# A decode kernel's output row moved from four spread partitions to eight neighbouring ones

## The chip, the cores and the metric

The kernel runs on one core of one Trainium2 chip. Times are device microseconds (us) of one execution. Ratios are the mean time of one kernel's fast runs over the mean of the other's fast runs of the same rounds, so they are not quite the ratio of the medians quoted beside them. A span in a profile runs from the first to the last instruction and is about 1.3 us shorter than the device time of the same run. Single executions of one kernel differ by about 0.3 us. So each claim rests on two things: the medians of repeated runs, and the last few microseconds of the trace, where single durations repeat to about 0.02 us.

## The reference

One token of attention with 32 query heads over a cache of 65,536 positions, a small gated MLP, and a gate that mixes the two. What matters here is the last line: two products that end in the same 1024 outputs.

```python
def reference(A_x, A_k_cache, A_v_cache, A_wq, A_wo, B_x, B_w_in, B_w_sp, B_b_sp, B_w_out, gate_w):
    ...                                   # q = x @ wq, softmax(q k / sqrt(128)) v per head
    a = o.reshape(1, 1, 4096) @ A_wo      # A_wo is 4096 x 1024, 8 MB
    b = (z1 * g_b) @ B_w_out              # the MLP, 1792 x 1024
    return g * a + (1 - g) * b            # 1024 numbers in bf16
```

## The kernel before

All inputs are loaded once, in one stream of large loads on the SP queue: keys, values, and at the very end `A_wo` in pieces. The last three pieces hold five, two and one of eight rows of weights per partition. The engines are written for the raw language, with semaphores planned by a small recorder.

The output `o @ A_wo` is one row, so a matmul uses one column of weights (`ovec`, one value per partition) and streams the rows of `A_wo` past it. The code places the matmuls in four groups of 32 columns (`tile_position`), and the groups run side by side: in the trace the four matmuls of a row of weights start within 0.02 us of each other, and the next row follows after 0.11 us at full clock, 0.21 at half. Each group writes to its own 32 partitions of PSUM (`fb[32*q:32*q+1]`). The kernel gives each group a quarter of the 1024 outputs, so the sums end on partitions 0, 32, 64 and 96, with 256 columns each:

```python
for c in range(c0, c1):                       # rows of weights per partition
    for q in range(4):                        # four column groups
        o = DO * (c - c0) + QW * q            # QW = 256
        e.matmul(fb[32*q:32*q+1, 0:QW], ovec[:, 8*i+c:8*i+c+1], sl[:, o:o+QW], start=False, ...,
                 tile_position=(0, 32*q))
...
P("DVE", lambda e: e.tensor_copy(orow[0:97, :], fb[0:97, 0:QW]), w=["orow", "fb"])   # PSUM -> SBUF
store()
# the store's source: four partitions, every 32nd
osrc = bass.AP(tensor=arena, offset=OFF["OROW"], ap=[[32 * NA, 4], [1, QW]])
```

The same store is also issued once early, of zeros, just before the last load. The MLP's product is summed in rows of 512 into `ob`, and four small fp32 matmuls with the vector `e4` spread it into the four rows of `fb`.

## Time and profile before

| | before |
|---|---|
| median of the runs | 382.32 us (382.23 to 382.40, six runs) |
| bytes read | 162 MB, 426 GB/s over the span |
| busy: DMA, PE, DVE | over 90% in 39 of 40 slices, 60%, 54% |
| last landing of weights to end of span | 2.60 us |

The page of the profile, its header and the rows of 40 equal slices. A digit is the busy share of a slice in tenths:

```profile
span 381.1 us, 2468 instructions
...
PE 229.2 (60%) x1383; PEld 55.5 (15%) x793; DVE 204.5 (54%) x162; ACT 22.2 (6%) x23; POOL 7.5 (2%) x35
...
DMA  9999999999999999999999999999999999999995
...
q8 instruction: 8, 0.13, 0.1%
```

DMA is full from the first slice to the last but one. No compute engine is near that. So the load stream sets the time, and a change after it can only win in what follows the last landing. The last line is the queue that the page calls "instruction" (packets, MB, share of the span of all 16 engines): eight packets.

The chain of work that ended last, for the last 15 us (start us, length us, what):

```profile
345.52 31.08 DMA arena<-in_A_wo_dram
...
376.74 1.73 PE fbt L718 x28
378.47 0.03 issue
378.50 0.41 PE fbt L718 x4
...
379.00 0.42 DVE arena L724
```

The timeline of the same stretch (start us, length us, engine, line, operation, operands, count, and in brackets the idle time before it and what ended it), with the early store of zeros first:

```profile
346.47 0.63 SPq L354 DMA_DIRECT2D out_dram<-arena  x1
...
378.50 0.09 PEld L718 LDWEIGHTS fbt<-arena 128*1 128x1 bf16 x4 [0.52 <-DMA arena<-in_A_wo_dram]
379.00 0.42 DVE L724 CAST arena<-fbt 97x256 bf16<-97x256 f32 x1 [9.98 <-PE fbt L718]
379.45 0.54 SPq L354 DMA_DIRECT2D out_dram<-arena  x1
```

So the tail reads like this. The last row of weights lands at 378.45 (from the record of landings). PE starts at 378.50 and releases DVE, which copies from 379.00 for 0.42 us. SP issues the store at 379.45 for 0.54 us. The store lands at 381.05. That last stretch is SP's final wait (waited for, us in total, times, longest):

```profile
SPq L121 <- DMA out_dram<-arena: 1.1, 1, 1.1
```

PE's clock in the last two 3.4 us windows was half speed (columns: busy time and count of PE, weight loads, DVE, ACT, POOL; PEclk; DMA share; GB/s):

```profile
374.10:377.60 3.50, 1.67 (x40) 0.78 (x28) 0.00 (x0) 0.00 (x0) 0.00 (x0) 0.51 0.78 315
377.60:381.00 3.40, 1.25 (x20) 0.19 (x12) 0.42 (x1) 0.00 (x0) 0.00 (x0) 0.50 0.02 6
```

### The profile page before, as it was taken

Reading aid. Unit: us, or ns where it says so; the run is one execution under the profiler, and the core shown is the slowest. Engines: PE = TensorE matmul, PEld = TensorE weight load, DVE = VectorE, ACT = ScalarE, POOL = GpSimd, SP = SyncE. Lnnn points to the kernel's source line nnn. Section 1 sums busy time; section 2 is a strip of 40 time slices with the busy share of each in tenths; the row PEclk is TensorE's granted clock in tenths of the full one; section 3 lists DMA queues with packets and bytes.
Section 4 is the critical chain, followed back from the end, with each engine's and each line's share of the span. In section 5 each row is a group of like instructions: output and inputs, shape, how many; then the busy total and the mean of one; then the engine's idle time right before and its main releaser. Section 6 shows DMA issues by size and latency. Waiting matters only on the chain.

```text
span 381.1 us, 2468 instructions
## 1 busy us (share of the span) xinstructions
PE 229.2 (60%) x1383; PEld 55.5 (15%) x793; DVE 204.5 (54%) x162; ACT 22.2 (6%) x23; POOL 7.5 (2%) x35
## 2 busy tenths in 40 slices
PE   0050487566558924893887238952995984549373
PEld 0010011111111200121111001220121111212031
DVE  3111596778489525956882249745875871402020
ACT  1000000010420000002000000022000000220000
POOL 4000000000000000000000000000000000000000
PEclk9997599698959975999798858985998896959776
DMA  9999999999999999999999999999999999999995
GB/s 440 434 433 413 426 387 437 440 492 420 428 433 392 426 442 440 433 420 433 454 428 440 440 440 440 421 433 440 392 420 439 457 433 426 426 408 433 423 430 223
DMA packets 4237, 162.15 MB, mean 426 GB/s; under 512 B 508, under 2 KB 516, under 8 KB 772
## 3 DMA queue, kind: packets, MB, share of 16 engines
q1 hardware_dynamic: 4192, 162.01, 98.7%
q8 instruction: 8, 0.13, 0.1%
q10 hardware_dynamic: 36, 0.00, 0.0%
q14 instruction: 1, 0.01, 0.0%
HBM read 162.01 MB, written 0.00 MB: 425 GB/s over the span
## 4 chain that ended last, share of the span: by engine, by line
DMA 63%; DVE 18%; PE 17%; issue 1%; ACTq 0%; SPq 0%; DVEq 0%
DMA arena<-in_A_k_cache_dram 41%; DVE arena L490 15%; DMA arena<-in_A_v_cache_dram 10%; DMA arena<-in_A_wo_dram 8%; PE scp L250 5%; DMA arena<-in_B_b_sp_dram 5%; PE scp L252 5%; PE obt L250 3%; PE obt L252 3%; DVE arena L527 1%; PE fbt L718 1%; ACTq L276 0%; DVE arena L563 0%; DVE arena L561 0%; SPq L377 0%
## 5 line engine op out<-in xcount | busy, mean ns | idle before, releaser
L490 DVE STREAM_TRANSPOSE arena<-arena 128x2048 f32<-128x2048 f32 x64 | 142.8, 2283 | 45.9 <-DMA arena<-in_A_k_cache_dram 31.3
L250 PE MATMUL scp<-arena 128*128 128x512 bf16 x256 | 108.9, 425 | 84.9 <-DVE arena L490 84.9
L252 PE MATMUL scp<-arena 128*128 128x512 bf16 x256 | 107.7, 421 | 0.0
L250 PE MATMUL obt<-arena 128*64 128x512 bf16 (+2 forms) x334 | 62.8, 416 | 21.3 <-DMA arena<-in_A_v_cache_dram 21.3
L252 PE MATMUL obt<-arena 128*64 128x512 bf16 (+2 forms) x334 | 61.9, 410 | 0.0
L250 PEld LDWEIGHTS scp<-arena 128*128 128x128 bf16 x256 | 26.9, 105 | 194.4 <-issue 99.5
L527 DVE STREAM_TRANSPOSE arena<-arena 128x2048 bf16<-128x2048 bf16 x7 | 16.2, 2311 | 31.3 <-PE obt L252 29.1
L250 PEld LDWEIGHTS obt<-arena 128*64 128x64 bf16 (+1 forms) x334 | 18.3, 113 | 74.5 <-issue 56.9
L522 ACT ACTIVATE arena<-arena 128x2048 bf16<-128x2048 f32 x8 | 16.0, 2003 | 218.1 <-DVE arena L519 195.0
L507 DVE TENSOR_SCALAR_CACHE_REDUCE arena<-scp 128x2048 f32<-128x2048 f32 x8 | 18.3, 2292 | 16.0 <-PE scp L252 16.0
L568 PE MATMUL mbt<-arena 128*128 128x128 bf16 x16 | 2.2, 286 | 13.6 <-DVE arena L563 13.6
L530 DVE STREAM_TRANSPOSE arena<-arena 128x1024 bf16<-128x1024 bf16 x2 | 2.5, 1245 | 12.7 <-PE obt L252 12.7
L718 PE MATMUL fbt<-arena 128*1 128x256 bf16 x128 | 6.6, 370 | 4.1 <-DMA arena<-in_A_wo_dram 4.0
L556 DVE RECIPROCAL arena<-mbt 128x1 f32<-128x1 f32 x4 | 0.6, 140 | 15.7 <-PE mbt L551 15.7
L478 POOL COPY arena<-arena 32x32 bf16<-32x32 bf16 x16 | 3.3, 204 | 236.3 <-PE scp L252 210.9
L519 DVE TENSOR_REDUCE arena<-mbt 128x1 f32<-128x32 f32 x4 | 0.8, 192 | 13.3 <-PE mbt L516 13.3
L420 PE MATMUL scp<-arena 8*128 8x1 bf16 x8 | 0.6, 197 | 10.8 <-DVE arena L415 10.8
L425 PE MATMUL mbt<-arena 1*128 1x2 bf16 x1 | 0.2, 158 | 10.4 <-DMA arena<-in_B_b_sp_dram 10.4
L724 DVE CAST arena<-fbt 97x256 bf16<-97x256 f32 x1 | 0.4, 425 | 10.0 <-PE fbt L718 10.0
L427 DVE COPY arena<-mbt 128x2 f32<-128x2 f32 x1 | 0.2, 159 | 10.4 <-PE mbt L425 10.4
L718 PEld LDWEIGHTS fbt<-arena 128*1 128x1 bf16 x128 | 3.3, 103 | 7.2 <-DMA arena<-in_A_wo_dram 3.4
L415 DVE TENSOR_TENSOR arena<-arena 8x1024 bf16<-8x1024 bf16 x1 | 1.2, 1211 | 4.9 <-DMA arena<-in_A_x_dram 4.9
(88 smaller groups left out, 48.9 us busy)
## 6 DMA issues: line engine op xcount, KB each, us to landing
arena<-in_A_k_cache_dram SPq DMA_DIRECT2D x6, 4096.0 KB, 33.2
arena<-in_A_v_cache_dram SPq DMA_DIRECT2D x2, 4096.0 KB, 26.9
arena<-in_B_w_in_dram SPq DMA_DIRECT2D x1, 7168.0 KB, 31.0
arena<-in_A_wo_dram SPq DMA_DIRECT2D x3, 2048.0 KB, 34.4
arena<-in_B_w_out_dram SPq DMA_DIRECT2D x1, 3584.0 KB, 21.8
arena<-in_A_wo_dram SPq DMA_DIRECT2D x1, 1280.0 KB, 31.1
arena<-in_A_wo_dram SPq DMA_DIRECT2D x1, 512.0 KB, 31.8
arena<-in_A_wo_dram SPq DMA_DIRECT2D x1, 256.0 KB, 31.3
```

Of the source, the lines that this page charges most:

```text
L250: return e.matmul(*a, **kw)
L252: one = e.matmul(*a, **kw).ins
L415: P("DVE", lambda e: e.tensor_tensor(vw(xm, 0, [[128, 8], [1, 128]], 0, 8), vw(xrow, 0, [[0, 8], [1, 128]], 0, 8), vw(idb, 0, [[1, 8], [0, ...
L478: P("POOL", lambda e, pb=pb: e.tensor_copy(vw(qpad, 24 + 32 * pb, [[QP, 4], [1, 8]], 32 * pb, 32), vw(qall, 8 * g, [[32, 4], [1, 8]], 32 * ...
L490: P("DVE", lambda e: e.transpose(ktb(i).bitcast(F32), sl[:, 4096 * p:4096 * (p + 1)].bitcast(F32)), r=keys[4 * p:4 * p + 4], w=[("kt", i % ...
L507: P("DVE", lambda e: e.tensor_scalar(scs(j), scp[:, :], 0.0, None, op0=ALU.add, op1=ALU.max, accum_out=maxc[:, j:j + 1]), w=[("sc", j % 2) ...
L519: P("DVE", lambda e: e.tensor_reduce(gcol(g, K_NB), mb[:, 0:32], AXX, ALU.min), w=[("nb", g), "mb"])
L522: P("ACT", lambda e: e.activation(psb2, scs(j), ACTF.Exp, bias=gcol(j // 2, K_NB), scale=SCALE, accum_out=lp[:, j:j + 1]), r=[("sc", j % 2 ...
L527: P("DVE", lambda e: e.transpose(ptsb2, psb2), r=["psb"], w=[("ptsb", 0), ("ptsb", 1)])
L530: P("DVE", lambda e: e.transpose(ptsb(n), ab("PSB", 1024, 1024 * (n % 2))), r=["psb"], w=[("ptsb", n % 2)])
L568: ins = e.matmul(mb[:, 0:128], sel[:, 128 * c:128 * (c + 1)], osc[:, 128 * c:128 * (c + 1)], start=(c == 0), stop=(c == 3))
L718: ins = e.matmul(fb[32 * q:32 * q + 1, 0:QW], ovec[:, 8 * i + c:8 * i + c + 1], sl[:, o:o + QW], start=False, stop=(i == 3 and c == 7), ti ...
```

## The change

The intent: end with eight rows of 128 columns on eight partitions that follow one another, 28 to 35, so that the copy is short and the store is a block of neighbours. These partitions lie in two column groups, so only two groups of PE work; each matmul takes a weight load of 32 columns. A window into a zero-padded vector (`ovz`) puts the one useful column at the right place. To make up for PE's lost half, the first half of `A_wo` is summed in rows of 512 over four groups and spread into the eight rows later, and ten filler matmuls (`spin`) are meant to keep PE busy so that its clock stays up.

```diff
-    QW = DO // 4
+    NW = 8
+    QW = DO // NW
+    W0 = 32 - NW // 2
...
-    osrc = bass.AP(tensor=arena, offset=OFF["OROW"], ap=[[32 * NA, 4], [1, QW]])
+    osrc = orow[W0:W0 + NW, :]
...
+    SLOTS = []
+    for h in range(NW // 2):
+        SLOTS += [(h, 0, W0 + h), (NW // 2 + h, 1, h)]        # (which 128 outputs, column group, row in it)
+    def wo_rows(i):                     # first half of A_wo: rows of 512, four groups, into scp
...
+    def wo_piece(i, c0=0, c1=8):        # second half: rows of 128 straight into fb
+        ...
+                for s, b, j in SLOTS:
+                    z = 31 + 32 * (8 * i + c) - j
+                    ins = e.matmul(fb[32 * b:32 * (b + 1), 0:QW], ovz[:, z:z + 32], sl[:, o:o + QW], ...,
+                                   tile_position=(0, 32 * b))
...
     out_first(3)
+    wo_rows(0)
     out_rest(3)
+    wo_rows(1)
+    spin(4)
+    spread(scp, [KSC(0)], False)        # ACT copy 97x1024, then eight fp32 matmuls
+    spin(3)
+    wo_piece(2)
+    spin(3)
+    for c0, c1 in WO_CUT:
+        wo_piece(3, c0, c1)
-    P("DVE", lambda e: e.tensor_copy(orow[0:97, :], fb[0:97, 0:QW]), w=["orow", "fb"])
+    P("DVE", lambda e: e.tensor_copy(orow[0:W0 + NW, :], fb[0:W0 + NW, 0:QW]), w=["orow", "fb"])
```

## The prediction

> **What bounds the kernel now.** The page's header and its row of 40 slices: 162 MB at a mean of 426 GB/s, DMA 9 tenths busy in every slice but the last, PE 60%, DVE 54%. The chain of waits over the last 80 us is almost only DMA: value cache until 339.5, output weights until 376.6. So the load queue sets the time, and only what follows the last landing can be saved. Read from the landings and instruction times: the last piece of the output weights (one of eight rows) lands at 378.45 us; its four 128*1 by 256 matmuls start at 378.50 and release DVE at 378.94 (0.41 us, clock at half); the 97x256 copy takes 0.42; the store is issued at 379.45 for 0.54 and lands at 381.05. The tail from last landing to end is 2.6 us of 381.1.

> **What the change does.** No byte loaded moves, and no load waits for anything new: the queue was filled up to its last load at 347 us. So the last landing should stay at 378.45, give or take 0.15.
> - Copy: 36x128 instead of 97x256. Between the 128x2 copy (0.16 us) and the 97x256 one (0.425) lies about 1.05 ns per column; estimate 0.29 us, 0.13 less. On the chain.
> - Store: eight rows of 256 bytes instead of four of 512[...]. The eight-row load of x took about the same issue time (0.58 us against 0.54). Estimate 0, at most 0.1 either way.
> - PE, output weights: only two of four column groups work now, each row costs 4x128 columns in turn instead of 256: 0.21 us warm, 0.43 cold (before 0.11 and 0.21, both seen in the spacing of the matmuls). For rows 0 to 15 the sums over 512 columns keep four groups busy, so they cost the same as before; added are one 97x1024 ScalarE copy (1.02 us, as the one at 99.6), eight fp32 matmuls and ten filler matmuls of 512 columns. All of that fits into the waits for landings at 368.6, 373.5 and 376.6: off the chain.

> **Clock.** From the clock record against PE's occupancy in its 3.41 us windows: a fast window is followed by a fast one if PE was over about half busy, a slow one is lifted only above about 0.75. [...] Before, the last two windows were slow (occupancy 0.35 and 0.46). With the fillers I expect about 0.8 in each from 367 on, so the last matmuls run fast: rows 0 to 4 end near 377.7, rows 5 and 6 follow their landing at 377.83, the last row needs 0.38 to 0.45 after 378.45: equal to before. If the clock stays low the backlog at the end is about 1 us. [...]

> **Sum.** 382.36 - 0.13 (copy) + 0.07 (mean of the backlog risks) = 382.3 us; range 381.8 to 382.8. Faster by over 2%: 0.005; within 2%: 0.985; slower by over 2%: 0.01.

> **What would show it.** Last landing within 0.2 of 378.45; clock 1.0 in the windows from about 371 on; copy near 0.29 us; output matmuls of 32x128 waiting for DMA before each of the last three pieces. Wrong if: PE has a backlog at the last landing (no DMA wait before the last eight matmuls), the clock is 0.5 there, or the store lands over 0.2 us later or earlier than 1.05 us after its issue.

The sum came to 382.3 us. A backlog of about 0.5 us is one of the risks in the 0.07. What the traces show for the rest: in before's clock record every stretch but the last is a multiple of 3.41 us long (the windows; their counts are in "Why the prediction was right or wrong"), the rows of weights started 0.11 us apart at full clock and 0.21 at half, and the store was four packets of 512 bytes, after the change eight of 256. The trace names no DMA engine for a packet.

## The result, and the profile after

The changed kernel took 381.81 us (median of six, 381.72 to 381.98) against 382.32: ratio 0.9987, 95% interval 0.9974 to 1.0. By the 2% measure that is the same. The gain is 0.5 us, about eight times the 0.06 that the prediction summed up to.

The page after:

```profile
span 380.5 us, 2581 instructions
...
PE 231.1 (61%) x1449; PEld 57.7 (15%) x836; DVE 204.1 (54%) x162; ACT 23.2 (6%) x24; POOL 8.4 (2%) x37
...
DMA  9999999999999999999999999999999999999996
...
q8 instruction: 9, 0.15, 0.2%
```

The stream is as full as before. PE has 109 more records of matmuls and weight loads, and one more instruction packet came. The chain after:

```profile
376.65 1.77 PE fbt L705 x56
378.42 0.01 issue
378.43 0.42 PE fbt L705 x8
...
378.94 0.28 DVE arena L768
```

and the timeline after, again with the early store of zeros first:

```profile
345.73 0.38 SPq L359 DMA_DIRECT2D out_dram<-arena  x1
...
378.43 0.23 PEld L705 LDWEIGHTS fbt<-arena 128*32 128x32 bf16 x8 [0.18 <-DMA arena<-in_A_wo_dram]
378.94 0.28 DVE L768 CAST arena<-fbt 36x128 bf16<-36x128 f32 x1 [10.80 <-PE fbt L705]
379.25 0.31 SPq L359 DMA_DIRECT2D out_dram<-arena  x1
```

SP's final wait after:

```profile
SPq L121 <- DMA out_dram<-arena: 0.9, 1, 0.9
```

The clock is now full in the last two windows:

```profile
374.10:377.60 3.50, 3.41 (x100) 2.60 (x94) 0.00 (x0) 0.00 (x0) 0.00 (x0) 1.00 0.78 313
377.60:381.00 3.40, 1.22 (x37) 0.85 (x31) 0.28 (x1) 0.00 (x0) 0.00 (x0) 1.00 0.04 12
```

Set side by side, from the instruction records and the record of landings:

| us | before | after | difference |
|---|---|---|---|
| last landing of weights | 378.45 | 378.39 | -0.06 |
| landing to start of copy (PE) | 0.55 | 0.56 | +0.01 |
| copy | 0.425 | 0.282 | -0.14 |
| store: issue | 0.535 | 0.309 | -0.23 |
| store: end of issue to landing | 1.06 | 0.89 | -0.17 |
| tail: last landing to landing of the store | 2.60 | 2.07 | -0.53 |

The copy saves what was forecast. The store saves 0.40 us, and nothing was forecast for it. PE, the place of nearly all the new code, gains nothing. The questions are what made the store cheaper, and whether the fillers and the rows of 512 do anything.

### The profile page after: what moved, and what is told of

The parts are those of the page before. It is cut to its first block, busy times and chain, and to the rows that moved or that the text cites. A ratio compares the mean times of both kernels' runs of the same rounds, so it can differ in the third digit from the quotient of the medians.

```text
span 380.5 us, 2581 instructions
## 1 busy us (share of the span) xinstructions
PE 231.1 (61%) x1449; PEld 57.7 (15%) x836; DVE 204.1 (54%) x162; ACT 23.2 (6%) x24; POOL 8.4 (2%) x37
## 4 chain that ended last, share of the span: by engine, by line
DMA 57%; PE 21%; DVE 19%; ACT 1%; issue 1%; ACTq 0%; SPq 0%; DVEq 0%
DMA arena<-in_A_k_cache_dram 34%; DVE arena L495 17%; DMA arena<-in_A_wo_dram 10%; DMA arena<-in_A_v_cache_dram 8%; PE scp L253 5%; DMA arena<-in_B_b_sp_dram 5%; PE scp L255 5%; PE obt L253 4%; PE obt L255 4%; DVE arena L532 1%; PE fbt L705 1%; PE fbt L653 1%; ACT arena L527 1%; ACTq L281 0%; SPq L382 0%
## 5 line engine op out<-in xcount | busy, mean ns | idle before, releaser
L253 PE MATMUL scp<-arena 128*128 128x512 bf16 (+1 forms) x275 | 110.7, 419 | 87.3 <-DVE arena L495 86.2
L255 PE MATMUL scp<-arena 128*128 128x512 bf16 (+1 forms) x279 | 110.5, 415 | 0.0
L253 PEld LDWEIGHTS scp<-arena 128*128 128x128 bf16 (+1 forms) x275 | 27.3, 103 | 196.5 <-issue 96.9
L705 PE MATMUL fbt<-arena 128*32 128x128 bf16 x128 | 4.1, 220 | 0.1
L460 DVE CAST arena<-obt 97x1024 bf16<-97x1024 f32 x1 | 1.2, 1225 | 5.0 <-PE obt L255 5.0
```

The source lines that it names most:

```text
L253: return e.matmul(*a, **kw)
L255: one = e.matmul(*a, **kw).ins
L705: ins = e.matmul(fb[32 * b:32 * (b + 1), 0:QW], ovz[:, z:z + 32], sl[:, o:o + QW], start=False, stop=(i == 3 and c == 7), tile_position=(0 ...
```

## The experiments

All kernels keep the loads as they are. "Tail" is again last landing of weights to landing of the store. Here are all the tails at once; the runs follow one by one.

| run | median us | ratio to before | last landing | landing to copy | copy | issue | flight | tail |
|---|---|---|---|---|---|---|---|---|
| before | 382.32 | | 378.45 | 0.55 | 0.42 | 0.54 | 1.06 | 2.60 |
| the change | 381.81 | 0.9987 | 378.39 | 0.56 | 0.28 | 0.31 | 0.89 | 2.07 |
| e1 four neighbours | 381.81 | 0.9986 | 378.39 | 0.55 | 0.42 | 0.29 | 0.90 | 2.18 |
| e3 before, four neighbours | 381.87 | 0.9986 | 378.30 | 0.55 | 0.42 | 0.28 | 0.91 | 2.19 |
| e4 every 16th | 382.26 | 0.9996 | 378.47 | 0.46 | 0.29 | 0.60 | 1.06 | 2.44 |
| e5 before, every 2nd | 382.50 | 1.0002 | 378.44 | 0.55 | 0.42 | 0.62 | 1.07 | 2.68 |
| e6 no fillers | 381.83 | 0.9989 | 378.42 | 0.56 | 0.28 | 0.31 | 0.89 | 2.07 |
| e7 no rows of 512 | 383.10 | 1.0017 | 379.49 | 0.56 | 0.28 | 0.31 | 0.90 | 2.07 |
| e8 sixteen neighbours | 385.18 | 1.0070 | 378.47 | 3.21 | 0.22 | 0.34 | 1.25 | 5.04 |
| e9 80 more early | 381.83 | 0.9994 | 378.27 | 0.56 | 0.28 | 0.31 | 0.90 | 2.08 |
| e10 150 more early | 383.03 | 1.0020 | 380.02 | 0.56 | 0.28 | 0.31 | 0.90 | 2.08 |
| e11 two queues | 381.99 | 0.9990 | 378.20 | 0.49 | 0.29 | 0.28 | 0.88 SP, 1.07 ACT | 2.15 |
| e12 four, plain | 382.01 | 0.9993 | 378.38 | 0.57 | 0.42 | 0.29 | 0.90 | 2.20 |

"Flight" is from the end of the issue to the landing. The sums lack about 0.03 us between copy and issue.

### What makes the store cheap: rows, neighbours, or the rest of the program

**e1, the change with four neighbouring rows of 256.**

```diff
-    NW = 8
+    NW = 4
```

> The changed kernel with four neighbouring partitions of 256 columns instead of eight of 128 (right result). Read: from the last weight landing to the end. Theory E (the number of rows of the store[...] sets its cost): store issue about 0.53 us and issue end to landing about 1.06, as before the change; whole tail about 2.07 + 0.39 + 0.13 = 2.6 us. Theory N (neighbouring partitions instead of every 32nd set it): issue about 0.31, flight about 0.90, the copy back at about 0.42; tail about 2.2. Theory P (nothing about the store, the rest of the changed program sets it): as N.

The timeline of e1:

```profile
378.94 0.42 DVE L768 CAST arena<-fbt 34x256 bf16<-34x256 f32 x1 [10.94 <-PE fbt L705]
379.38 0.29 SPq L359 DMA_DIRECT2D out_dram<-arena  x1
```

The issue was 0.29 and the flight 0.90, with the copy back at 0.42: theory E (the number of rows) falls, N and P stand. The time was 381.81, like the change itself; the 0.1 us of the longer copy is within the spread of the runs.

**e2 and e3, the kernel before with only its store's source changed.** Results are wrong, because only every 32nd partition holds sums.

```diff
-    osrc = bass.AP(tensor=arena, offset=OFF["OROW"], ap=[[32 * NA, 4], [1, QW]])
+    osrc = orow[28:36, 0:128]      # e2; a second line, cut here, makes rows of 128 on the side of out
+    osrc = orow[28:32, :]          # e3
```

> The kernel before, only its two stores read eight neighbouring partitions of 128 columns (wrong result on purpose: all but one of those rows hold no sums). Theories E and N: issue about 0.31 and flight about 0.90 in place of 0.535 and 1.06, the rest of the tail as before; the time falls by about 0.4 us. Theory P: issue stays at 0.53, the time does not move.

> The kernel before, its stores read four neighbouring partitions of 256 columns (wrong result on purpose). Theory E: issue 0.53, flight 1.06, time as before. Theory N: issue 0.31, flight 0.90, time lower by about 0.4 us. Theory P: as E.

The times of e2's four fast runs had a median of 382.02 us. Its profiled execution, 588 us long, is no evidence for the tail, though its store shows 0.31 us of issue too. In it, matmuls of 512 columns mostly started 0.62 us apart, where the kernel before has 0.22 at full clock; the clock's record, which holds no event for that execution, said full speed (1.000). The page of that execution, and its timeline:

```profile
span 586.8 us, 2468 instructions
```

```profile
585.60 0.31 SPq L354 DMA_DIRECT2D out_dram<-arena  x1
```

e3 is the clean one. The timeline of e3:

```profile
378.34 0.09 PEld L718 LDWEIGHTS fbt<-arena 128*1 128x1 bf16 x4 [0.53 <-DMA arena<-in_A_wo_dram]
378.85 0.42 DVE L724 CAST arena<-fbt 97x256 bf16<-97x256 f32 x1 [11.01 <-PE fbt L718]
379.30 0.28 SPq L354 DMA_DIRECT2D out_dram<-arena  x1
```

PE and the copy are exactly the kernel before, yet the issue fell from 0.54 to 0.28 and the final wait from 1.1 to 0.9 us. Its time was 381.87 against 382.34. One line of address pattern gives 0.47 of the 0.5 us (0.41 in the tail alone), without any change on PE. Theory P falls as well.

The store still has four rows here. The record of landings shows one early update of the semaphore (380.41 in before) and four later ones (380.99 to 381.05), in e3 as in before; with eight rows it is one and eight. Four or eight rows make no difference here: the change has an issue of 0.31 and a flight of 0.89, e1 0.29 and 0.90.

**e4, the change with its rows on every 16th partition.** All four column groups work, two rows in each.

```diff
-    osrc = orow[W0:W0 + NW, :]
+    osrc = bass.AP(tensor=arena, offset=OFF["OROW"], ap=[[16 * NA, NW], [1, QW]])
...
-    for h in range(NW // 2):
-        SLOTS += [(h, 0, W0 + h), (NW // 2 + h, 1, h)]
+    for k in range(NW // 4):
+        SLOTS += [((NW // 4) * b + k, b, 16 * k) for b in range(4)]
...                                   # the copy takes 113 partitions
```

> The changed kernel, its eight rows of 128 columns on every 16th partition (two in each of four column groups) instead of on eight neighbours (right result). Theory E: issue 0.31, flight 0.90. Theory N: issue 0.53, flight 1.06, so 0.4 us slower than the change. The four column groups halve the time of a row of weights (0.24 to about 0.12 us), and the last eight matmuls should release the copy about 0.1 us earlier: under E the tail is about 1.97 us, under N about 2.35.

The timeline of e4:

```profile
378.51 0.12 PEld L707 LDWEIGHTS fbt<-arena 128*32 128x32 bf16 x8 [0.38 <-DMA arena<-in_A_wo_dram]
...
378.93 0.29 DVE L770 CAST arena<-fbt 113x128 bf16<-113x128 f32 x1 [11.05 <-PE fbt L707]
379.25 0.60 SPq L359 DMA_DIRECT2D out_dram<-arena  x1
```

The eight weight loads take half the time (0.12 us against 0.23 in the change), and the copy starts 0.46 us after the landing instead of 0.56. But the issue takes 0.60 and the flight 1.06: tail 2.44, time 382.26. PE's gain of 0.1 is outweighed by the store's loss of 0.46. This is theory N again, this time with eight rows and a right result.

**e5, how near is near.** The kernel before, rows from partitions 0, 2, 4 and 6.

```diff
-    ... ap=[[32 * NA, 4], [1, QW]])
+    ... ap=[[2 * NA, 4], [1, QW]])
```

> The kernel before, its stores read four rows of 256 columns from every second partition, 0, 2, 4 and 6 (wrong result on purpose). It asks what 'neighbouring' means. Theory N1 (the partitions have to follow one another without a gap): issue about 0.53 and flight about 1.06, tail 2.6 as before. Theory N2 (the rows only have to lie in one group of 32 partitions, or close together): issue about 0.29 and flight about 0.90, tail 2.2.

Its store in the timeline:

```profile
379.44 0.62 SPq L354 DMA_DIRECT2D out_dram<-arena  x1
```

A gap of one partition costs no less than a gap of 31: issue 0.62, flight 1.07, time 382.50 (a little above before). N1 holds. The rows need not lie in one group of 32: e1's partitions 30 to 33 and the change's 28 to 35 cross the border of two groups and are fast (issue 0.29 and 0.31, flight 0.90 and 0.89).

Why a gap costs this much was not shown. The traces show where the time is: the first data packet started 1.17 us after the start of the issue in before, 1.23 in e4 and 1.25 in e5, against 0.78 in the change and 0.77 in e3. The packets themselves took 15 to 32 ns in these five runs. So the time passes before the first packet, not in moving the data. No run looks inside that.

Two rivals to "the gap as such" were not run. All slow stores (before, e4, e5) start at partition 0, all fast ones at partition 24 or later. One load speaks against the start as the cause: `gate_w` goes to the neighbouring partitions 0 to 7, and its issue took 0.28 us in the trace of before. The other rival is the way the program is built: whatever the build does differently for a store with a gap goes together with the gap in every run, so it stays open whether the chip is slower with a gap or the built store is another one.

### The fillers

**e6, the change without `spin`.**

```diff
-    spin(4)
-    spin(3)          # all three calls
```

> The changed kernel without its ten filler matmuls (right result). If the fillers are what keeps the PE clock up: clock 0.5 at the last landing, a row of weights takes 0.43 us, PE is about 1 us behind when the last row lands (no DMA wait before the last eight matmuls), time up by 0.7 to 1.3 us against the change. If the clock stays up without them, the tail is 2.07 us as in the change.

The windows of e6's clock at the end, and the line of `wo_piece(2)` in its timeline:

```profile
372.30:375.70 3.40, 3.11 (x54) 2.60 (x52) 0.00 (x0) 0.00 (x0) 0.00 (x0) 0.50 0.98 409
375.70:378.90 3.20, 2.96 (x90) 2.44 (x86) 0.00 (x0) 0.00 (x0) 0.00 (x0) 1.00 0.42 162
```

```profile
373.48 3.02 PE L705 MATMUL fbt<-arena 128*32 128x128 bf16 x64 [0.29 <-DMA arena<-in_A_wo_dram]
```

The clock was at full speed (1.00 in the window from 375.70) at the last landing all the same, and the tail is 2.07. Without the fillers `wo_piece(2)` ran at half clock and lasted 3.02 us instead of 1.96. It thereby kept PE busy for 92% of the window before, and full speed followed, as it did after every half-speed window that busy in the trace of before (81% and more, 14 windows; none up to 71% was followed by it). The fillers bought nothing here in the median (381.83). One of the five runs took 382.49, though. The windows fall differently in the two executions compared (one began at 374.15 us in the profile of before, at 372.87 in that of the change), so it stays open whether the fillers protect against an unlucky one.

### The rows of 512

**e7, the first half of the weights straight into the eight rows.**

```diff
-    wo_rows(0)
+    wo_piece(0)
     out_rest(3)
-    wo_rows(1)
+    wo_piece(1)
     spin(4)
-    spread(scp, [KSC(0)], False)
     spin(3)
```

> The changed kernel with the first half of the output weights summed like the second, straight into rows of 128 (no rows of 512, no second spread; right result). My theory: that half has 5 us of room before the landing at 373.4, 16 rows at 0.24 us need 3.8 us, so nothing on the chain moves: tail 2.07, time as the change within 0.15 us. Rival: the rows of 512 are needed to keep up: PE late at 376.5 and at the last landing, tail longer by 0.3 us or more.

Both theories missed. The timeline of e7:

```profile
376.63 1.75 PE L705 MATMUL fbt<-arena 128*32 128x128 bf16 x56 [0.48 <-DMA arena<-in_A_wo_dram]
379.53 0.23 PEld L705 LDWEIGHTS fbt<-arena 128*32 128x32 bf16 x8 [1.33 <-DMA arena<-in_A_wo_dram]
...
380.04 0.28 DVE L767 CAST arena<-fbt 36x128 bf16<-36x128 f32 x1 [11.19 <-PE fbt L705]
```

PE was early, as I had thought: it waited 1.3 us for the last piece of weights. The tail is 2.07, as I had thought. But the last piece landed 1.1 us late, and the time was 383.10, in each of five runs between 382.91 and 383.22. The record of landings shows how: of its sixteen parts, fifteen landed between 376.48 and 378.32, and one at 379.49.

The page of e7 has 1529 matmuls and 932 weight loads for PE, 176 records more than the change. The queue that the pages call "instruction" (q8) moves packets of 16,384 bytes, in before some 35 to 55 us apart in the middle of the run, mostly 1.0 to 1.1 us each. I call such a packet an instruction block. Their number went up with PE's records: eight with 1383 matmuls and 793 weight loads (before), nine with 1449 and 836 (the change), ten with 1609 and 996 (e8). These are its last packets, in us from the start of the span, and the end of the weights' stream:

```
run      last instruction packet   weights' packets after it            last landing
before   371.81 to 372.88          many                                 378.45
change   378.13 to 379.09          none                                 378.39
e7       376.95 to 378.02          seven of 2 KB, 378.01 to 379.05      379.49
e8       377.48 to 378.49          none                                 378.47
e9       377.73 to 378.78          none                                 378.27
e10      377.78 to 378.85          three of 2 KB, 378.83 to 379.49      380.02
e11      377.66 to 378.75          none                                 378.20
```

In e7 an instruction block came while the last weights were on their way, and the last seven packets of weights moved only after it: the first at 378.01, when the block ended at 378.02. The other fifteen parts were down by 378.32. The packets after the block took up to 0.23 us each, where the other last ones took 0.08, which adds to the delay. That the block and the late part shared one of the core's DMA engines is my reading; no trace here names the engine of a packet.

**e8, sixteen rows of 64.**

```diff
-    NW = 8
+    NW = 16
```

> The changed kernel with sixteen neighbouring rows of 64 columns (right result). Store over neighbours, so issue and flight stay near 0.31 and 0.90; the copy of 64 columns takes about 0.22 us (0.06 less). A matmul of 64 columns costs 27 ns if only the columns count: tail 2.0. [...]

The timeline of e8:

```profile
376.69 1.17 PE L705 MATMUL fbt<-arena 128*32 128x64 bf16 x68 [0.39 <-DMA arena<-in_A_wo_dram]
380.02 1.40 PEld L705 LDWEIGHTS fbt<-arena 128*32 128x32 bf16 x60 [2.29 <-issue]
```

The 27 ns is an eighth of the 0.215 us between starts of 512-column matmuls at full clock in the trace of before, so an estimate. It held: 128 matmuls of 64 columns took 2.04 us in `wo_piece(2)` and started every 15 ns on average over the two groups, near the 13.5 that 27 ns for the columns would give. The kernel lost 3.4 us against the change for another reason. PE stopped for 2.2 us in the middle of its last work, although all weights had landed by 378.47, and with no wait of the program to show for it ("issue"). An instruction packet ran from 377.48 to 378.49, and PE came back only 1.5 us after it; whether the two are connected was not shown. The store missed my figure too: its issue took 0.34 us, and of its sixteen parts fifteen landed within 0.99 us of the end of the issue, but the last after 1.25, not 0.90. No run explains that.

**e9 and e10: move the instruction blocks alone.** One weight load and 79 (149) tiny matmuls are added at 30 us, where PE waits for keys. From there on the same work lies 80 (150) instructions later in the stream.

```diff
+    def pad(e):
+        for k in range(79):            # e10: 149
+            ins = mm(e, k > 0, tb[:, 0:8], idb, idb[:, 0:8], start=True, stop=True)
+        return ins
+    P("PE", pad, r=["idb"], w=[KTB])
```

> The changed kernel with one weight load and 79 matmuls of eight columns added at about 30 us, where PE waits for keys (right result). It moves everything after by 80 PE instructions in the instruction stream and nothing else. Theory F (in the run without rows of 512 the ninth 16 KB block of instructions was fetched at 376.95 on a DMA engine that still had weights to bring, and those landed 1.1 us late): the ninth fetch, at 378.13 in the change, moves to about 377.0; the last landing goes from 378.4 to about 379.4, the tail stays 2.07, the time rises by about 1.1 us. Rival W (the rows of 512 matter for the work PE does at the end, the landing at 379.49 was chance): last landing 378.4, time as the change.

> As the run with 80 more, with 150 more PE instructions at about 30 us (right result). Theory F: the ninth fetch comes at about 375.1 and takes the same engine's time, so the last landing is late by up to 1.1 us again (by less if that engine can catch up). Rival W: no change of the landing or of the time.

The DMA engine in theory F is the reading given under e7; what these two runs can show is the time of the block and the landing.

The timeline of e10:

```profile
376.75 1.75 PE L711 MATMUL fbt<-arena 128*32 128x128 bf16 x56
380.06 0.23 PEld L711 LDWEIGHTS fbt<-arena 128*32 128x32 bf16 x8 [1.73 <-DMA arena<-in_A_wo_dram]
...
380.57 0.28 DVE L774 CAST arena<-fbt 36x128 bf16<-36x128 f32 x1 [12.58 <-PE fbt L711]
```

e10 came out as theory F says. With the rows of 512 in place, the same program after 30 us and a tail of 2.08, one part of the last piece landed at 380.02 while the fifteen others were there by 378.25. The time was 383.03, in all four runs over 382.9. So the landing in e7 was not chance, and not PE's work (theory W).

My figures for when the block comes were wrong. I expected 377.0 in e9 and 375.1 in e10; it came at 377.73 and 377.78. And e9 did not come out as theory F forecast: the weights landed at 378.27, the median of its runs is 381.83. The time of the block alone does not decide, since e9's came before e10's, and those of e11 (377.66) and e8 (377.48) came earlier still without a late landing. What differs in the profiles is whether weights were left behind it: seven packets in e7, three in e10, none in the others. One of e9's six runs took 383.52, which would fit a block with weights behind it, but that run has no profile. The change itself has the block at 378.13, 0.16 us after its last packet of weights ended, and none of its six runs is over 382.0. It wins a race by a small margin. The rows of 512 keep the instruction count lower; e7 shows what they are worth in this program, 1.2 to 1.3 us.

### Versions meant to be better

**e11, two rows in each of four groups and two stores of four neighbours, from SP and from ACT.**

```diff
+    halves = [("SP", "out", 30, 0), ("ACT", "out2", 94, 4)]
...                                   # store() issues one DMA for each half
+    SLOTS = [(2 * b + h, b, (30, 0, 30, 0)[b] + h) for h in range(2) for b in range(4)]
```

> A version meant to beat both: rows of 128 columns in all four column groups, two neighbouring rows on each side of partitions 32 and 96, stored as four neighbours from the SP queue and four from the ACT queue at once (right result). PE needs half the time for a row, so the copy starts about 0.46 us after the last landing as with every 16th partition (0.55 in the change); copy 0.29, issue about 0.29 to 0.38, flight 0.90: tail about 1.97 us against 2.07, time lower than the change by about 0.1 us, if the second queue costs nothing. If two stores disturb each other the tail is 2.1 us or more.

The SP store landed 0.88 us after the end of its issue, the ACT store, issued at the same time, after 1.07. PE gained 0.06 and the second queue lost more than that: tail 2.15, time 381.99. It misses its aim.

**e12, four neighbours and nothing else.** No fillers, no rows of 512.

```diff
-    NW = 8
+    NW = 4
-    wo_rows(0)            # and wo_rows(1), spread, all spin calls
+    wo_piece(0)           # and wo_piece(1)
```

> The least of the change that should keep its gain: four neighbouring partitions of 256 columns, no rows of 512, no fillers (right result). PE then issues as many matmuls as before the change, so the ninth instruction block should not come before the last landing. If neighbouring partitions are what pays, the landing stays near 378.4, the tail is about 2.18 us as with four neighbours above (copy 0.42, issue 0.29, flight 0.90) and the time about 381.85, within 0.15 of the change. If fillers or rows of 512 are needed after all, PE is late at the last landing or the landing itself is late, and the time is over 382.3.

The timeline of e12:

```profile
376.28 2.56 PE L705 MATMUL fbt<-arena 128*32 128x256 bf16 x36
...
378.95 0.42 DVE L764 CAST arena<-fbt 34x256 bf16<-34x256 f32 x1 [10.37 <-PE fbt L705]
```

PE has the same number of records as before the change (1383 and 793), the ninth block did not come, the landing stayed at 378.38 and the tail was 2.20. The time, 382.01, is a little over the 381.85 that I expected, and its runs spread up to 382.22. In its profile PE worked without a pause into the last row, so it was just on time there; how it fares in an execution whose clock falls differently was not shown. No version beat the change; e1 equals it (ratio 0.9986 against 0.9987).

## Why the prediction was right or wrong

The range held the result at its very edge: 381.81 against a lower end of 381.8. That it held is luck, since the largest term of the gain was forecast as 0. The forecast of "within 2%" was right for the reason given: the load stream sets the time.

- **Last landing unchanged.** Right for this program: 378.39 against 378.45. The reason ("no load waits for anything new") was incomplete. e7 and e10 show that more PE instructions alone can make the last landing late by 1.1 to 1.6 us, without any load waiting for PE.
- **Copy, 0.13 less.** Right: 0.14.
- **Store, "Estimate 0, at most 0.1 either way".** This is the step that failed. The store became 0.40 us cheaper, 0.23 in the issue and 0.17 in the flight. I had looked at the number of rows, which e1 and e3 show to be without effect (issue 0.29 and 0.28 with four, 0.31 with eight). What counts is whether the partitions follow one another (e3, e4, e5: issue 0.28 without a gap, 0.60 and 0.62 with one; by the gap itself or by something in the build that goes with it), and the diff shows that in one line, that of `osrc`. My comparison also took the wrong sample. The load of x, at 0.58 us, was the first DMA of its queue. The next one of the same shape took 0.28, was in the same trace, and could have pointed to the right answer. My own test for the store, 0.2 us of room around a flight of 1.05, passes with 0.89: it left out the issue, where most of the gain was.
- **Last row on PE, 0.38 to 0.45 us, equal to before.** Right to 0.01: 0.46 in both. Half the column groups (two for four) and twice the clock (1.00 for 0.50) cancel.
- **Clock full at the end.** Right, but not because of the fillers: e6 has it without them. The rule that I used comes out of the trace of before, in windows of 3.41 us: a window at full speed was followed by full speed when PE was busy for 53% of it or more (52 windows), by half speed at 49% or less (15). The trace of the change has one at 41% that was followed by full speed, so the border is not sharp.
- **Backlog risk, +0.07.** It did not come. The weight loads of 32 columns hide behind the matmuls: 64 pairs of 128 columns took 1.96 us in `wo_piece(2)`, the weight loads 1.79 of it, which is 0.24 us for a row of weights, near the 0.21 estimated.
